# A warm-up of 9 wide multiplies becomes 7 wide and 26 narrow fp32 ones

## The chip, the cores and the metric

The kernel runs on one core of a Trainium2 chip. The metric is the device time of one execution in microseconds (us). Before the change the median of three runs is 491.01 us (488.01 to 491.92).

## The reference

Eight heads of a linear recurrence over 768 steps for 4 batches (head size 48), and then an MLP of 384 to 2048 to 384 with an exact GELU on each of the 3072 tokens:

```
for t in range(S):                       # per batch b and head h
    cur = outer(u * k_t, v_t)
    y_t = r_t @ (state + cur)
    state = w[:, None] * state + outer(k_t, v_t)
h = y @ w_in                             # (3072, 384) @ (384, 2048)
out = (0.5 * h * (1 + erf(h / sqrt(2)))) @ w_out
```

## The kernel before

The recurrence is cut into 6 chunks of 128 steps and 4 pairs of heads: 24 groups. Within a group the recurrence is a small causal attention. VectorE scales r and k by powers of the decay (`prepare`, L426); TensorE makes the scores (`scores` and `own`, L465, tile A), what the chunk adds to the state (`gains`, L476, tile UE), what the state before gives (`old`, L484, tile Y) and what the chunk's own values give (`new`, L502, tile Y); VectorE selects the causal half of the scores (L551, tile Am), advances the states (L521); ScalarE copies Y and the first states (L565, L532); GpSimd multiplies the keys by decays (L433, tile N). The first four groups, g0 to g3 here, run alone at the start, up to about 35 us. After that TensorE runs the MLP, 96 steps of 9 plus 9 multiplies of 512 columns (L649, tile Hp, and L692, tile O), and the other 20 groups between them.

The order on each engine is written out ahead by a planner (`Plan`): every piece of work has an engine, an estimated length in ns, a due time and the names that it reads and writes. Each engine then runs its list in that order. Where the planner sees TensorE idle in the first four groups, it puts multiplies by a tile of zeros (`heat`, L312) whose results nobody reads: 512 columns into UE up to the first `gains`, then 256 columns into AE. They are part of the fixed list.

At the very start stands `warm_up`, 9 multiplies of zeros with 512 columns (L314 to L320), followed by 4 of the planner's into UE; the first scores (g0) wait for VectorE's scaled T. Loads are issued on SyncE's queue, at most two or three at a time: T0, T1, N0, T2, N1, T3, w0 (the weights of the first MLP step), N2, N3, w1 and so on.

TensorE runs each multiply as a pair of instructions, a weight load (LDWEIGHTS) and the multiply (MATMUL). A multiply in plain fp32 appears in the trace as two pairs, so the 16 multiplies of `scores` are 32 pairs there; those of zeros and of the MLP are in fp32r and appear as one pair.

Of the kernel before, what the change touches and what calls it, by code (L numbers as in the profile page):

```python
# [9 lines left out]
F32 = mybir.dt.float32  # L10
# [10 lines left out]
B, H, S, D = 4, 8, 768, 48  # L21
# [17 lines left out]
LATER = 10 ** 7  # L39
FIRST, STEP, STEP_LAST = 23000, 8400, 3900  # L40
WEIGHT_AHEAD, GROUP_AHEAD, GROUP_DUE = 12500, 28000, 20000
HEATS, HEAT_NS, HEAT_ROOM = 9, 400, 300
LOADS = ("t0", "t1", "n0", "t2", "n1", "t3", "w0", "n2", "n3", "w1", "t4", "w2", "n4")
UNDERWAY, START = 2, 10
URGENT, WORTH = 1000, .5
# [6 lines left out]
class Plan:  # L52
# [9 lines left out]
    def add(self, eng, ns, at, fn, r=(), w=()):  # L62
        n = len(self.ops)
        deps = set()
        for x in r:
            deps.add(self.writer.get(x))
            self.readers.setdefault(x, []).append(n)
        for x in w:
            deps.add(self.writer.get(x))
            deps.update(self.readers.pop(x, ()))  # L70
            self.writer[x] = n
        deps -= {None, n}
        self.ops.append((eng, ns, at, fn, deps))
        self.reads.append(set(r))
# [77 lines left out]
def rwkv_gelu_mlp(tc, rkT, rkv, wuT, uN, wmlp, r, k, vT, w, u, out):  # L152
    nc = tc.nc
    with ExitStack() as ctx:
# [7 lines left out]
        def sb(shape, dt, name, pool=None):  # L162
            return (pool or wk).tile(shape, dt, name=name)
# [6 lines left out]
        AE = pso.tile([128, 2, 512], F32, name="AE")  # L170
# [34 lines left out]
        zeros = sb([128, 512], F32R, "zeros", pro)  # L205
# [4 lines left out]
        add, dma = plan.add, plan.dma  # L210
# [71 lines left out]
        for dst, src, x in ((diag2, diag, "diag"), (past2, past, "past")):  # L282
            for h in range(2):
                add("act", 280, LATER, lambda dst=dst, src=src, h=h: nc.scalar.copy(
                    out=dst[64 * h:64 * h + 64], in_=src[64 * h:64 * h + 64, 64 - 64 * h:128 - 64 * h]),
                    r=[x], w=[f"{x}2{h}"])
# [9 lines left out]
        for i in range(NP, NP + 2):  # L296
            for h in range(2):
                add("act", 520, LATER, lambda i=i, h=h: nc.scalar.copy(
                    out=flat2(T[i])[32:64, 512 * h:512 * h + 512], in_=zeros.bitcast(F32)[32:64]),
                    r=["zeros"], w=[f"T{i}"])  # L300
# [10 lines left out]
        def heat(dst, n=512):  # L311
            nc.tensor.matmul(dst, lhsT=zeros[:, 0:128], rhs=zeros[:, 0:n], start=True, stop=True)  # L312

        def warm_up():  # L314
            for n in range(HEATS):
                heat((A + [YU[:, 0], YU[:, 1]] + [AE[:, 0], AE[:, 1]])[n % 6])
            plan.filler = lambda: heat(UE[:, 1]), "O0", HEAT_NS, HEAT_ROOM
            plan.heat = lambda: heat(AE[:, 0, 0:U0], U0), 110, SHARE

        add("pe", 430 * HEATS, 10, warm_up, r=["zeros"], w=["H", "A0", "A1", "O0", "O1", "Y0", "Y1"])  # L320

# [628 lines left out]
```

## Time and profile before

| what | value |
|---|---|
| median of 3 runs | 491.01 us |
| lowest and highest run | 488.01 and 491.92 us |
| profiled execution, its own time | 492.2 us |
| span of the profiled execution | 490.5 us |
| mean granted TensorE clock | 0.993 |
| busy: TensorE multiplies, weight loads | 479.8 us, 389.8 us |
| busy: VectorE, ScalarE, GpSimd | 265.9, 174.9, 64.8 us |
| instruction packets on DMA queue 8 | 42, 0.69 MB |

The span is what the profile covers, from the first to the last instruction; 1.7 us of the execution's own time lie outside it. In the chain of waits, "issue" is time in which an engine waited for nothing that the profile shows. A granted clock of 1.00 is 2.4 GHz, 0.50 is 1.2 GHz.

### The profile page before, as it was taken

To read this page: it belongs to the slowest core of one execution; us is meant where nothing else is said; L and a number is where in the kernel's file an instruction comes from. 1 tells how busy PE (TensorE), PEld (TensorE's weight loads), DVE (VectorE), ACT (ScalarE), POOL (GpSimd) and SP (SyncE) were. 2 spreads that over 40 slices of the span, in tenths; PEclk is the share of its full clock that TensorE was granted. 3 is DMA by queue.
4 is the path that set the end of the run, shared out by engine and by line. 5 is a ranking of instruction groups with operands and counts; after the bars stand their busy time and mean duration, and the time that the engine had idled before them with its cause. 6 is when DMAs were issued, how large, how long until landed. Compare 5 with 4: busy or idle time off the path is not lost.

```text
span 490.5 us, 11672 instructions
## 1 busy us (share of the span) xinstructions
PE 479.8 (98%) x5094; PEld 389.8 (79%) x5094; DVE 265.9 (54%) x432; ACT 174.9 (36%) x353; POOL 64.8 (13%) x85
## 2 busy tenths in 40 slices
PE   8799999999999999999999999999999999999996
PEld 6687787878888888778878888888888887888885
DVE  7478989876636636536545645554545423322223
ACT  6288889853132232231321331331421311211111
POOL 5200000002202022112022021120120200000000
PEclk9799999999999999999999999999999999999999
DMA  8674576513312312303113403123313000100002
GB/s 221 210 234 170 176 268 198 193 37 113 91 31 62 92 34 77 131 0 94 43 49 94 143 3 94 33 60 93 103 42 94 1 11 13 66 0 0 1 0 71
DMA packets 13193, 42.25 MB, mean 86 GB/s; under 512 B 2160, under 2 KB 2544, under 8 KB 13136
## 3 DMA queue, kind: packets, MB, share of 16 engines
q1 hardware_dynamic: 13136, 41.43, 28.1%
q8 instruction: 42, 0.69, 0.6%
q14 instruction: 15, 0.12, 0.1%
HBM read 34.74 MB, written 4.72 MB: 80 GB/s over the span
## 4 chain that ended last, share of the span: by engine, by line
PE 96%; DVE 1%; issue 1%; DMA 1%; ACT 0%; SPq 0%; DVEq 0%
PE Hp L649 41%; PE O L692 40%; PE A L465 3%; PE Y L484 3%; PE Y L502 2%; PE AE L312 2%; PE Y L476 2%; PE Y L692 1%; DMA T<-in_rkT_dram 1%; DVE T L426 0%; PE Y L515 0%; PE UE L476 0%; DVE Am L551 0%; DVE wa L865 0%; PE A L312 0%
## 5 line engine op out<-in xcount | busy, mean ns | idle before, releaser
L649 PE MATMUL Hp<-xx,wh 128*128 128x512 f32 x576 | 166.6, 396 | 0.5 <-ACT gf L679 0.3
L679 ACT ACTIVATE gf<-Hp 128x512 f32<-128x512 f32 x96 | 57.4, 598 | 229.2 <-PE Hp L649 223.6
L680 DVE CAST gh<-gf 128x512 fp32r<-128x512 f32 x95 | 45.5, 479 | 168.4 <-ACT gf L679 167.6
L649 PEld LDWEIGHTS Hp<-xx,wh 128*128 128x128 f32 x576 | 106.8, 188 | 25.8 <-ACT gf L679 1.2
L649 PE MATMUL Hp<-xx,wl 128*128 128x512 f32 x288 | 83.3, 396 | 0.0
L692 PE MATMUL O<-gh,wh 128*128 128x512 f32 (+1 forms) x285 | 81.9, 394 | 0.0
L692 PE MATMUL O<-gl,wh 128*128 128x512 f32 (+1 forms) x285 | 80.7, 390 | 0.0
L692 PE MATMUL O<-gh,wl 128*128 128x512 f32 (+1 forms) x285 | 80.6, 390 | 0.0
L681 DVE TENSOR_TENSOR gl<-gf,gh 128x512 fp32r<-128x512 f32 x95 | 73.2, 771 | 9.7 <-DVE gh L680 0.5
L649 PEld LDWEIGHTS Hp<-xx,wl 128*128 128x128 f32 x288 | 54.0, 188 | 12.9
L692 PEld LDWEIGHTS O<-gh,wh 128*128 128x128 f32 x285 | 52.5, 188 | 12.6 <-issue 0.3
L692 PEld LDWEIGHTS O<-gl,wh 128*128 128x128 f32 x285 | 52.5, 188 | 11.6
L692 PEld LDWEIGHTS O<-gh,wl 128*128 128x128 f32 x285 | 52.5, 188 | 11.6
L456 ACT ACTIVATE Am<-diag,cs 128x64 f32<-128x64 f32 x120 | 31.7, 337 | 29.8 <-DVE cs L451 29.8
L430 POOL TENSOR_TENSOR Nb<-Nb 128x384 f32<-128x384 f32 x15 | 15.9, 1063 | 127.9 <-DMA Nb<-in_rkv_dram 112.7
L433 POOL TENSOR_TENSOR Nb<-Nb,WN 128x384 f32<-128x384 f32 x20 | 21.5, 1073 | 56.3 <-DMA Nb<-in_rkv_dram 32.0
L426 DVE TENSOR_TENSOR Tb<-Tb,E 112x1024 f32<-112x1024 f32 x20 | 25.2, 1258 | 3.2 <-DMA Tb<-in_rkT_dram 3.0
L521 DVE SCALAR_TENSOR_TENSOR Sb<-Sa,E,Y 48x192 f32<-48x192 f32 x40 | 16.5, 413 | 14.0 <-ACT xx L565 7.7
L493 POOL MEMSET turn<- 1x1 f32 x19 | 1.7, 89 | 129.2 <-PE Y L484 129.2
L565 ACT CAST xx<-Y 112x512 fp32r<-112x512 f32 (+1 forms) x18 | 10.6, 587 | 22.4 <-PE Y L476 16.4
L551 DVE COPY_PREDICATED Am<-past,A 128x512 f32<-128x512 uint32 x24 | 17.7, 736 | 0.4
L448 POOL TENSOR_TENSOR Nb<-Nb,u_sb 128x384 f32<-128x384 f32 x15 | 17.3, 1155 | 0.1
(109 smaller groups left out, 401.1 us busy)
## 6 DMA issues: line engine op xcount, KB each, us to landing
raw<-in_wmlp_dram SPq DMA_DIRECT2D x16, 768.0 KB, 4.3
Nb<-in_rkv_dram SPq DMA_DIRECT2D x15, 576.0 KB, 4.0
Tb<-in_rkT_dram SPq DMA_DIRECT2D x40, 192.0 KB, 3.5
out_dram<-raw SPq DMA_DIRECT2D x5, 768.0 KB, 3.8
Nb<-in_rkv_dram SPq DMA_DIRECT2D x5, 384.0 KB, 3.7
xx<-x SPq DMA_DIRECT2D x30, 64.0 KB, 2.3
N<-in_rkv_dram SPq DMA_DIRECT2D x4, 384.0 KB, 6.4
T<-in_rkT_dram SPq DMA_DIRECT2D x2, 448.0 KB, 4.8
```

What stands on the lines that cost most here:

```text
L426: add("dve", sdve(1024), LATER if g.gi else -10 ** 5, lambda: nc.vector.tensor_tensor(out=flat, in0=flat, in1=E[:, 0, g.p].rearrange("l h ...
L430: add("pool", pool(DM), LATER, lambda: nc.gpsimd.tensor_tensor(out=g.n[:, 0], in0=g.n[:, 0], in1=g.n[:, 1], op=ALU.mult), r=[g.K], w=[g.R])
L433: it = nc.gpsimd.tensor_tensor(out=g.kn, in0=g.kn, in1=WN[:, g.p].rearrange("s j d -> s (j d)").unsqueeze(1).to_broadcast([C, NB, 2 * D]), ...
L448: add("pool", pool(DM), LATER, lambda: nc.gpsimd.tensor_tensor(out=g.n[:, 0], in0=g.n[:, 0], in1=u_sb[:, g.p, :].unsqueeze(1).to_broadcast ...
L456: add("act", sact(HALF) + 60, LATER, lambda x=x, b=b: nc.scalar.activation(out=g.am[:, x, b, :], in_=diag2, func=AF.Copy, scale=g.sums[:, ...
L521: return nc.vector.scalar_tensor_tensor(out=g.s[h + 1][quarter(1 - x)], in0=g.s[h][l], scalar=E[l, 1, g.p, h, MID:MID + 1], in1=gained(g, ...
L551: add("dve", 722, LATER, lambda: nc.vector.copy_predicated(out=g.am, mask=mask.bitcast(U32).unsqueeze(1).unsqueeze(1).to_broadcast([C, 2, ...
L649: nc.tensor.matmul(O[3], lhsT=wt[j][:, 0, k_ * 128:(k_ + 1) * 128], rhs=x[:, a, k_, :], start=start and k_ == ks[0], stop=stop and k_ == k ...
L679: add("act", 600, LATER, lambda: nc.scalar.activation(out=gf, in_=O[3], func=AF.Gelu), r=["H"], w=["gf"])
L680: add("dve", sdve2(512), LATER, lambda: nc.vector.tensor_copy(out=high, in_=gf), r=["gf"], w=[GH])
L681: add("dve", sdve(512), LATER, lambda: nc.vector.tensor_tensor(out=low, in0=gf, in1=high.bitcast(F32), op=ALU.subtract), r=["gf", GH], w=[GL])
L692: nc.tensor.matmul(bank(dst)[:, a:b], lhsT=wt[j][:, 1, d * 128:(d + 1) * 128], rhs=gt[:, a:b], start=(j == 0 and n == 0), stop=(j == NJ - ...
```

## The change

Two of the nine wide multiplies go; after the other seven come 26 multiplies by the same zeros, read as fp32, with 64 rows, 64 weight columns and 16 moved columns, each in one of four quarters of the array, into AE. The planner is told 40 ns for each. No other code changes.

```diff
-HEATS, HEAT_NS, HEAT_ROOM = 9, 400, 300
+HEATS, SMALL, HEAT_NS, HEAT_ROOM = 7, 26, 400, 300
...
         def warm_up():
             for n in range(HEATS):
                 heat((A + [YU[:, 0], YU[:, 1]] + [AE[:, 0], AE[:, 1]])[n % 6])
+            z = zeros.bitcast(F32)
+            for n in range(SMALL):
+                i, j = (slice(64 * (n // k % 2), 64 * (n // k % 2) + 64) for k in (1, 2))
+                nc.tensor.matmul(AE[j, n % 2, 0:16], lhsT=z[i, 0:64], rhs=z[i, 0:16], start=True, stop=True)
             plan.filler = lambda: heat(UE[:, 1]), "O0", HEAT_NS, HEAT_ROOM
             plan.heat = lambda: heat(AE[:, 0, 0:U0], U0), 110, SHARE
 
-        add("pe", 430 * HEATS, 10, warm_up, r=["zeros"], w=["H", "A0", "A1", "O0", "O1", "Y0", "Y1"])
+        add("pe", 430 * HEATS + 40 * SMALL, 10, warm_up, r=["zeros"], w=["H", "A0", "A1", "O0", "O1", "Y0", "Y1"])
```

TensorE's list from the first multiply to the second group's `own`, before (T_102 and T_103 are T of g0 and g1, KB their keys times u, N_110 the keys and values of g0):

```order
1 L312 MATMUL A<-zeros 128x512 x2
2 L312 MATMUL Y<-zeros 128x512 x2
3 L312 MATMUL AE<-zeros 128x512 x2
4 L312 MATMUL A<-zeros 128x512 x2
5 L312 MATMUL Y<-zeros 128x512
6 L312 MATMUL UE<-zeros 128x512 x4
7 L465 MATMUL A<-T_102 64x64 x16
8 L312 MATMUL UE<-zeros 128x512
9 L355 MATMUL AE<-ident,E 128x112 x4
10 L465 MATMUL A<-T_102,KB_108 64x64 x16
11 L312 MATMUL UE<-zeros 128x512 x3
12 L476 MATMUL UE<-N_110 48x48 x16
```

The same list now (the lines after the edit are four higher):

```order
1 L312 MATMUL A<-zeros 128x512 x2
2 L312 MATMUL Y<-zeros 128x512 x2
3 L312 MATMUL AE<-zeros 128x512 x2
4 L312 MATMUL A<-zeros 128x512
5 L320 MATMUL AE<-zeros 64x16 x26
6 L312 MATMUL UE<-zeros 128x512 x4
7 L469 MATMUL A<-T_102 64x64 x16
8 L312 MATMUL UE<-zeros 128x512
9 L359 MATMUL AE<-ident,E 128x112 x4
10 L469 MATMUL A<-T_102,KB_108 64x64 x16
11 L312 MATMUL UE<-zeros 128x512 x3
12 L480 MATMUL UE<-N_110 48x48 x16
```

Only the warm-up's rows differ. Every later row of TensorE, down to the last, stands in the same order with the same number of zero multiplies, and so do all rows of VectorE, ScalarE, GpSimd and SyncE.

The place where the first four groups go on, g1's scores to the zero multiplies behind g0's `new`, as it stands now (it is the same before, with lines four lower):

```order
13 L469 MATMUL A<-T_103 64x64 x16
14 L469 MATMUL A<-T_103,KB_109 64x64 x16
15 L488 MATMUL Y<-T_102,Sb 48x64 x8
16 L506 MATMUL Y<-Am_116,N_110 48x64 x16
17 L312 MATMUL AE<-zeros 128x256 x8
```

In the trace each of the first four rows is twice as many pairs (32, 32, 16, 32). They stand 100 instructions further from the start than before.

## Rows read from the trace of the kernel before

**Rows 1.** The page: busy time, granted clock in 40 slices, instruction packets

```profile
PE 479.8 (98%) x5094; PEld 389.8 (79%) x5094; DVE 265.9 (54%) x432; ACT 174.9 (36%) x353; POOL 64.8 (13%) x85
...
PEclk9799999999999999999999999999999999999999
...
q8 instruction: 42, 0.69, 0.6%
```

**Rows 2.** Chain of waits, first 46 us: start us, us, what

```profile
11.09 1.16 PE A L465 x64
12.25 0.44 PE Y L484 x16
...
12.78 0.55 PE Y L502 x24
13.33 3.46 issue
16.80 0.46 PE Y L502 x8
17.26 2.00 PE AE L312 x8
19.26 1.92 PE A L465 x64
21.18 1.36 PE AE L312 x5
22.54 0.81 PE UE L476 x32
23.35 1.15 PE AE L312 x8
...
27.60 0.36 PE UE L476 x32
27.95 1.39 PE AE L312 x10
```

**Rows 3.** Stretches: length, busy us (count) by engine, granted clock, DMA share, GB/s

```profile
8.00:10.00 2.00, 1.92 (x39) 1.22 (x37) 1.87 (x4) 1.33 (x3) 1.02 (x1) 1.00 0.99 246
...
16.00:18.00 2.00, 1.20 (x12) 1.06 (x13) 0.00 (x0) 0.67 (x2) 0.00 (x0) 0.59 0.07 29
18.00:20.00 2.00, 2.00 (x35) 1.78 (x37) 0.00 (x0) 0.72 (x2) 0.87 (x1) 0.50 0.49 126
```

**Rows 4.** DMA queues from 14.5 to 15.6 us: packets, MB, share

```profile
q8 instruction: 1, 0.02, 5.6%
```

**Rows 5.** DMA queues from 18 to 19.5 us

```profile
q8 instruction: 1, 0.02, 5.9%
```

**Rows 6.** Stretches from the start to each of two stops of TensorE

```profile
0.00:13.50 13.50, 11.07 (x221) 8.41 (x221) 10.25 (x25) 8.41 (x19) 7.09 (x14) 1.00 0.83 231
...
0.00:106.20 106.20, 99.57 (x1623) 81.00 (x1624) 84.13 (x132) 80.21 (x122) 14.91 (x25) 0.97 0.62 195
```

**Rows 7.** Chain of waits, 100 to 110 us

```profile
106.02 0.39 issue
```

**Rows 8.** TensorE in order of time, first 12 us

```profile
4.29 1.05 PE L312 MATMUL A<-zeros 128*128 128x512 f32 x2
5.15 0.63 PE L312 MATMUL Y<-zeros 128*128 128x512 f32 x1
...
6.86 0.69 PE L465 MATMUL A<-T 48*64 48x64 f32 x32
...
8.31 0.69 PE L465 MATMUL A<-T,KB 48*64 48x64 f32 x32
...
10.06 0.57 PE L476 MATMUL UE<-N 64*48 64x48 f32 x32
```

**Rows 9.** VectorE in order of time, from 9 us

```profile
9.48 0.72 DVE L551 COPY_PREDICATED Am<-diag,A 128x512 f32<-128x512 uint32 x1
```

**Rows 10.** GpSimd in order of time, from 8 us

```profile
19.13 1.97 POOL L433 TENSOR_TENSOR N<-N,WN 128x384 f32<-128x384 f32 x2 [6.14 <-DMA N<-in_rkv_dram]
```

## Prediction
> **What bounds the kernel now.** I read the page's busy times first: TensorE multiplies for 98% of the span, on one core, with a granted clock of 0.9 or more in every slice but one, the second [rows 1]. From some 38 us on nothing but TensorE's own work stands on the chain, so time is to be had only ahead of that, and there the clock slice says where to look: about 12 to 25 us. The chain of waits for that stretch [rows 2] shows one large hole. g0's `new` (L502) has done 24 of its 32 pairs at 13.33 us and does nothing for 3.46 us, waiting for nothing that the profile names, in the middle of 32 identical multiplies. It goes on at 16.80. Behind that hole the granted clock is down: 0.59 on average from 16 to 18 us and 0.50 from 18 to 20 [rows 3]; the page's third slice, which begins at 24.5 us, has it up again [rows 1]. So nearly all of the work from 16.80 to about 24 us runs at the 1.2 GHz level.
>
> What ends the hole? The DMA queues by stretch show the first packet of the instruction queue between 14.5 and 15.6 us [rows 4], and TensorE starts 1.2 us after that. I read the hole as TensorE out of instructions. The counts support it. At the stop TensorE has run 221 pairs, 442 instructions [rows 6]. A second, short stop of the same kind, 0.39 us, stands at 106.02 us, again inside a run of equal multiplies [rows 7], after 1623 multiplies and 1624 weight loads [rows 6]. The difference is 2805 instructions, 11 times 255, and with the few waiting instructions that these counts leave out a block of 256 fits. A packet is 0.69 MB / 42 = 16.4 KB [rows 1]. So blocks end at a fixed count of instructions, and TensorE stops at such an end where the next block is not there.
>
> **The change part by part.** *Removed:* two wide multiplies, 0.43 us each by their starts (4.29 to 5.15 for two, [rows 8]): 0.86 us of TensorE. *Added:* 26 fp32 multiplies, 52 pairs. No row has a pair with 16 columns; the nearest are the 64-column pairs of the scores, 64 in 1.92 us at the low clock and in 1.16 us at the high one [rows 2], so 30 or 18 ns. The warm-up's wide multiplies take 0.43 us for 512 columns, the pace of the low level, though the clock reads 1.00 [rows 6, 8]; so I take 30 ns: 1.56 us, net +0.70 us; at 18 ns +0.08 us. Since the four multiplies behind them then meet a clock that has risen, I put g0's scores 0.3 us later (0 to 0.7). That is off the path: the first selection on VectorE, which the chain goes through, starts at 9.48 us [rows 9] and the scores that it needs end at 9.00 [rows 8], a cover of 0.48 us. Cost 0, or 0.2 at the upper end. If the clock stays low until g0 is done, the cover is gone and it costs about 1 us.
>
> *Moved:* 52 - 2 = 50 pairs, 100 instructions, so every block's end falls 50 pairs earlier in the work. The stop after pair 221 becomes one after what was pair 171. Counting the list (13 + 32 + 1 + 4 + 32 + 3 + 32 + 32 = 149 up to g1's scores), that is the 22nd pair of g1's `own`: at 11.09 + 54/64 x 1.16 = 12.07 us [rows 2].
>
> *When the next block comes* decides all. The stop's row alone doesn't say when it was asked for. I take it that a block is asked for when TensorE is through with the block before the one it is in, 128 pairs earlier: pair 93, the 8th of g0's `gains`, at 10.2 us [rows 8]. From there to 16.80 are 6.6 us, with the DMA engines full. The second packet fits: TensorE enters the next block at 16.80 and the packet lies between 18 and 19.5 [rows 5] with the DMA engines nearly idle (0.07, [rows 3]); with the same 1.2 us behind it that makes 3.9 us. These are my bounds: 3.9 us idle, 6.6 us loaded.
>
> Now pair 93 is the 30th of g0's scores (63 + 30), at about 7.5 us. The block would be there between 11.4 and 14.1 us and is wanted at 12.07: a stop of **0 to 2.0 us**. The DMA share from 8 to 10 us is 0.99 [rows 3], so the loaded end is nearer; I take 1.2. The block after that is wanted 128 pairs on, at old pair 299, the end of g2's `own`. TensorE's work up to there at full clock is 0.18 + 0.44 + 0.09 + 0.73 + 1.11 + 1.16 = 3.7 us [rows 2], against 3.9 to 6.6: a stop of **0.2 to 2.9**. It is asked for at about 13.3, and the loads that fill the DMA engines were done by 16 (0.07 after that, [rows 3]); I take 1.0. The third has some 4.5 us of work ahead of it: 0 to 2.1, and I take 0, as the DMA engines are then lightly loaded.
>
> *What is at stake:* the 3.46 us, and the slow clock after it. At the low clock the steps from 16.80 to 24.50 take 0.46 + 2.00 + 1.92 + 1.36 + 0.81 + 1.15 = 7.70 us [rows 2]. At the high one: 0.18 (8/24 of 0.55), 1.11 (8/10 of 1.39), 1.16, 0.70, 0.36, 1.11 = 4.62 [rows 2]. That is 3.08 us; together **6.5 us**. Shorter stops should leave the clock up: up to 13.5 us TensorE was idle for 2.4 us in all, in pieces, and the clock stayed at 1.00 [rows 6]. From 24.5 on all moves rigidly, as TensorE has no gap. What is late next is GpSimd's N2 and N3, done from about 20.1 to 21.1 because their load was late [rows 10]; g2's `gains` would want N2 at 27.60 - 6.5 = 21.1, so just no wait. The later block ends move by 50 pairs too; the 0.39 us stop may go and another come, which I count as nothing (0.4 either way).
>
> *Sum:* -6.5 + 1.2 + 1.0 + 0 = -4.3 us on the profiled execution's 492.2 us (span 490.5 and 1.7 around it): 487.9. The median of the runs, 491.0, is 1.2 below the profiled one, and the lowest, 488.0, suggests that not every run pays the whole 6.5; by the median it would be 486.7. I say **487.5**.
>
> *A rule that speaks against it.* The hole lies at pair 221 while a 16.4 KB packet arrives [rows 4, 6]. The Trainium skill, "Runtime: NRT & Kernel Launch", section "Instruction fetch mechanics", says that instructions are refilled in blocks of 256 and that crossing a block's end is mostly hidden, because the sequencer issues slower than blocks arrive. The trace agrees with the block and not with "hidden": 256 small instructions here take some 3.7 us of work and a block 3.9 or more. By that rule the hole would have another cause and nothing would move: 491.
>
> **The rivals.**
> - *Clean:* both blocks arrive in time (idle latency). All 6.5 us go: 485.7 by the profiled time, 484.5 by the median; 485. For it: 3.9 us from 7.5 is 11.4. Against it: the DMA engines are at 0.83 from the start to 13.5 us [rows 6]. Chance 0.2.
> - *The hole only moves:* 2.0 us at g1's `own`, 1.0 later, and the clock falls all the same (3.1): 0.4 us saved, 490.6 to 491.8. For it: the loaded latency is the one that I have measured at that place. Against it: 2.0 us is much shorter than the stop after which the clock fell. Chance 0.18.
> - *Slower:* the early groups now eat blocks as fast as they come, so that each of three block ends stops TensorE at the loaded price, 2.0 + 2.9 + 2.1, with the low clock between them, 3.1: 10.1 against 6.5, so 3.6 us more, 494.6 to 495.8. It decides at g2's `own`: if the block asked for at about 14 us isn't there by 19. With the 1 us of an uncovered warm-up it passes 1%. Chance 0.06.
> - *Not what it says:* the stop isn't tied to the count (a wait for data that the profile does not name), or the narrow multiplies are fewer instructions than I count; nothing moves: 491. For it: no row shows when a block is asked for. Against it: the 2805 instructions between the two stops. Chance 0.06.
>
> **How the numbers follow.** My case, a smaller stop and no fall of the clock, has 0.5 and spans 486 to 489.5. About 1% (4.9 us, so 486.1 and 495.9) is what can be told from no change. Faster: the clean case, 0.2, and a third of mine, 0.17: 0.37. Slower: half of the slower case and some unseen trouble: 0.05. The rest, 0.58, within 1%. The range from 484.6 to 491.6 leaves out the slower case and the ends of the others.
>
> **What would show it.** In the changed kernel's chain the 3.46 us in L506 are gone, and "issue" of 0 to 2 us stands at g1's `own` (L469, 22 of 32 pairs), perhaps another at g2's; the first instruction packet lies at 10 to 13 us instead of 14.5; the granted clock is 1.00 from 14 to 24 us; the first MLP step (L653) starts some 4 us earlier. Wrong if a stop stays in g0's `new`, if the clock is at 0.50 anywhere from 13 to 24, or if g0's scores start after 7.6 us.

## The result, and the profile after

The changed kernel is slower: 494.96 us median against 490.08 us for the one before, run beside it; ratio 1.0095, 95% interval 1.0069 to 1.0121. The prediction was 487.5 us with a range of 484.6 to 491.6, so it was wrong in sign as well as in size. The profiled execution took 494.96 us, with a span of 493.2.

The page shows TensorE as busy as before, and its granted clock at 0.9 or more in all slices but the fifth, 49 to 62 us, where it was the second [rows 1]:

```profile
PE 481.8 (98%) x5144; PEld 390.2 (79%) x5144; DVE 266.4 (54%) x432; ACT 175.1 (35%) x353; POOL 64.5 (13%) x85
...
PEclk9999899999999999999999999999999999999999
```

5144 multiplies instead of 5094: fifty pairs more, as the change was read. The chain of waits of the first 36 us (start us, us, what) answers to [rows 2]:

```profile
4.93 1.61 PE AE L320 x52
6.54 2.00 PE UE L312 x4
8.54 1.06 PE A L469 x32
...
10.86 0.67 PE A L469 x32
...
16.97 1.15 PE A L469 x61
18.12 1.19 issue
19.30 0.33 PE A L469 x3
...
28.06 0.65 PE Y L506 x28
28.71 0.45 issue
29.16 0.32 PE Y L506 x4
...
33.52 1.63 PE Hp L653 x6
```

The 3.46 us in g0's `new` are gone. "Issue" now stands in g2's `own`, after 61 of 64 pairs, and in g2's `new`. The 26 narrow multiplies took 1.61 us as 52 pairs, and in TensorE's timeline g0's scores came at 8.47 instead of 6.86 us [rows 8], because the four wide multiplies behind the narrow ones still ran at about half pace (0.50 us each), as did the first 32 scores (1.06 us, where the next 32 took 0.67). The first MLP step begins at 33.52 us, 1.65 us earlier than in the chain of the profile before:

```profile
35.17 1.63 PE Hp L649 x6
```

All of that is lost again within 20 us. The chain from 48 us, the DMA queue from 48.2 to 49.3 us, and then the same MLP step in the chain before:

```profile
48.36 0.16 PE Y L480 x13
48.52 1.96 issue
50.48 0.48 PE Y L480 x19
...
52.12 3.61 PE Hp L653 x9
55.73 2.10 PE O L696 x9
```

```profile
q8 instruction: 1, 0.02, 5.2%
```

```profile
51.57 2.37 PE Hp L649 x9
53.94 2.10 PE O L692 x9
```

In the middle of a run of 32 equal pairs TensorE stops for 1.96 us, and an instruction packet arrives during the stop. After it nine MLP multiplies take 3.61 us; the same nine took 2.37 before. The stretches show why (length, busy us and count by engine, granted clock, DMA share, GB/s):

```profile
52.00:54.00 2.00, 1.94 (x6) 1.49 (x6) 1.97 (x4) 2.00 (x4) 0.00 (x0) 0.50 0.13 44
```

The granted clock is 0.50, 1.2 GHz, after the stop. And the end of the kernel differs. These are the last barrier's instructions, first those of before and then those of the changed kernel (engine, count, first and last start in us; each engine's second wait ends the kernel; TensorE's first DRAIN is its last instruction ahead of the first wait):

```profile
L947 ACTq EVENT_SEMAPHORE  x2: 17/17/17, 489.9 to 490.4; - x2
...
L947 PEldq EVENT_SEMAPHORE  x2: 51/51/51, 489.9 to 490.4; - x2
```

```profile
L951 PEldq DRAIN  x2: 8/10/13, 489.4 to 493.0; - x2
L951 ACTq EVENT_SEMAPHORE  x2: 17/17/17, 491.5 to 493.2; - x2
...
L951 PEldq EVENT_SEMAPHORE  x2: 51/51/51, 492.9 to 493.2; - x2
```

Before, ScalarE and TensorE come to it together, at 489.9 us. Now ScalarE is there at 491.5 and TensorE only at 492.9, 1.4 us later, though it has nothing left to compute. An instruction packet lies in the stretch from 489.5 to 491.5 us. So the profile's balance is -1.65 at the first MLP step, +1.96 for the stop, +1.5 for the clock behind it (the next products begin at 55.73 us against 53.94, so with the lead of 1.65 us 3.44 were lost there), about -0.4 for the stop at 106 us, which is gone [rows 7], and +1.4 at the barrier: +2.8, and the execution is 2.76 us longer than the profiled one before.

### The profile page after: what moved, and what is told of

Its sections match the earlier page's. It is cut to its first block, busy times and chain, and to the rows that moved or that the text cites. A ratio compares the mean times of both kernels' runs of the same rounds, so it can differ in the third digit from the quotient of the medians.

```text
span 493.2 us, 11772 instructions
## 1 busy us (share of the span) xinstructions
PE 481.8 (98%) x5144; PEld 390.2 (79%) x5144; DVE 266.4 (54%) x432; ACT 175.1 (35%) x353; POOL 64.5 (13%) x85
## 4 chain that ended last, share of the span: by engine, by line
PE 96%; issue 1%; DVE 1%; ACT 0%; DVEq 0%
PE Hp L653 42%; PE O L696 40%; PE A L469 4%; PE Y L488 3%; PE Y L506 2%; PE Y L480 2%; PE AE L312 1%; PE Y L696 1%; DVE Am L555 1%; PE UE L312 1%; PE A L312 1%; PE Y L519 0%; PE AE L320 0%; DVE wa L869 0%; PE UE L480 0%
```

## The experiments

Two theories stood against each other. **B (block ends):** TensorE's instructions come in blocks of 256; the 100 added ones move all block ends to other work, and those that now fall badly cost more than the first one gave. **W (warm-up):** the narrow multiplies keep the clock low at the start, and that is the loss. Each kernel was timed beside the one before.

### The order of the warm-up: 9 or 5 wide multiplies ahead of the narrow ones

```diff
-HEATS, SMALL, HEAT_NS, HEAT_ROOM = 7, 26, 400, 300
+HEATS, SMALL, HEAT_NS, HEAT_ROOM = 9, 26, 400, 300
```

> Nine wide multiplies come first, then the 26 narrow ones, then two wide: the same instructions as in the change and as many (100 more than before), only two wide ones moved ahead of the narrow ones. Theory B (block ends): the change loses at block ends of TensorE's instructions, so the stops stand at the same instructions as in the change (1.2 us in g2's own, 0.4 in g2's new, 2.0 in the gains near 48 us, 1.3 us at the last barrier), and the time is within 1 us of the change's 495.0 less what an earlier clock gives. Rival W (warm-up): the narrow multiplies hold the clock down (in the change it rose at 10.5 us instead of 6.1, and g0's scores began at 8.5 instead of 6.9). Then the clock rises near 6 us here, g0's scores begin near 7 and the first MLP step starts 1.5 to 2 us earlier than the change's 33.5; 493. If W alone were the cause of the loss, the time would be 490 or less.

Measured: 494.74 us, ratio 1.0083 (1.0056 to 1.0110). Its chain, 4 to 30 us, and a stretch behind the second stop:

```profile
12.59 0.32 issue
...
16.67 2.57 issue
19.24 0.47 PE A L469 x3
```

```profile
20.00:25.00 5.00, 5.00 (x89) 4.46 (x92) 2.62 (x5) 2.99 (x5) 0.85 (x1) 0.50 0.67 174
```

The 0.32 us stand in g1's `own`, 54 of 64 pairs in, where the prediction had put its first stop. The stop in g2's `own` is at the same instruction as in the change, 61 pairs in, and so is that near 50 us (2.13 us); but here the one in g2's `own` took 2.57 us and the clock fell to 0.50 behind it. The scores began earlier (7.31 us), and that was lost again: the first MLP step begins at 35.43 us. With five wide multiplies first:

```diff
-HEATS, SMALL, HEAT_NS, HEAT_ROOM = 7, 26, 400, 300
+HEATS, SMALL, HEAT_NS, HEAT_ROOM = 5, 26, 400, 300
```

> Five wide multiplies, 26 narrow ones, six wide: the same instructions as the change (7, 26, 4) and as the run with 9, 26, 2, in another order. Theory B: same stops at the same instructions, 495 as in those two. Rival W (the narrow multiplies hold the clock down, and that costs): the clock rises at 10 us or later and the time is 1 to 2 us above the run with nine wide ones first, 496 to 497. If the late clock of the change's profile was chance, it rises near 6 here.

Measured: 494.77 us, ratio 1.0090 (1.0054 to 1.0126). Its chain from 8 to 20 us:

```profile
8.54 1.06 PE A L469 x32
...
11.08 1.06 PE A L469 x32
...
17.92 1.08 PE A L469 x61
19.00 0.10 issue
19.09 0.33 PE A L469 x3
```

Here both halves of g0's scores run at half pace, 1.06 us for 32 pairs, where the change's second half took 0.67; but the block that g2's `own` needs is then there in time: 0.10 us of stop. Nine, seven and five wide multiplies first give 494.74, 494.96 and 494.77. So W is refuted as the cause of the loss; the run with 100 instructions at the first MLP step, below, loses as much with the warm-up of before (495.00 us). In these profiles, where the pace rises late TensorE comes later to block ends, and waits less there. How late the pace rises is not fixed by the order alone either: in the run below with the change's own warm-up TensorE's timeline (start us, us) has g0's first 32 scores in 0.69 us:

```profile
7.25 0.69 PE L469 MATMUL A<-T 48*64 48x64 f32 x32
```

### 100 or 256 instructions more, elsewhere

The warm-up of before, and narrow multiplies behind the first MLP step instead, 25 or 64 of them:

```diff
+        def pad(count):
+            z = zeros.bitcast(F32)
+            for n in range(count):
+                i, j = (slice(64 * (n // k % 2), 64 * (n // k % 2) + 64) for k in (1, 2))
+                nc.tensor.matmul(A[n % 2][j, 0:16], lhsT=z[i, 0:64], rhs=z[i, 0:16], start=True, stop=True)
...
-                        product1(x, j, n, (k_,), k_ == 0 and n == 0, k_ == 2 and n == 2) for n in range(3)],
+                        product1(x, j, n, (k_,), k_ == 0 and n == 0, k_ == 2 and n == 2) for n in range(3)] + [
+                        k_ == 2 and pad(25)],
```

> The warm-up of before; 25 narrow fp32 multiplies (50 pairs, 100 instructions) behind the first MLP step at about 37 us, where they cost some 0.9 us. Theory B: up to there all is as before (3.5 us stop in g0's new); after it the block ends stand as in the change: a stop of about 2 us in the gains near 50 us, none at 106 us, 1.3 us at the last barrier; 490.1 + 0.9 + 2.0 - 0.4 + 1.3 = 493.9, and up to 1.7 more where the clock falls after the stop. Rival W: no stop, 491.0.

Measured: 495.00 us, ratio 1.0103 (1.0069 to 1.0137). The chain of its profile near 47 us, and its last barrier:

```profile
47.34 0.16 PE Y L480 x13
47.50 2.19 issue
49.69 0.48 PE Y L480 x19
```

```profile
L958 ACTq EVENT_SEMAPHORE  x2: 17/17/17, 489.4 to 491.0; - x2
...
L958 PEldq EVENT_SEMAPHORE  x2: 51/51/51, 490.7 to 491.0; - x2
```

The stop stands behind the same 13 of 32 pairs as in the change, the one at 106 us is gone, and TensorE is 1.3 us late at the barrier. Nothing of the warm-up was touched. The multiplies themselves take 0.92 us in its chain.

> As the run with 100 more instructions at the first MLP step, but 64 narrow multiplies: 128 pairs, 256 instructions, one whole block. They cost 128 x 17 ns = 2.2 us. Theory B: all block ends fall on the same work as before, so the 0.4 us stop in the gains stands again (at about 108 us), no 2 us stop near 50 us and nothing at the last barrier: 492.3, less than with 100 instructions. Rival (more instructions cost more, wherever the blocks end): slower than the run with 100, 495 or more.

Measured, with `pad(64)`: 493.34 us, ratio 1.0068 (1.0047 to 1.0089). Near 107 us:

```profile
107.24 0.25 PE Y L480 x18
107.49 0.39 issue
107.88 0.39 PE Y L480 x11
```

With one whole block more the stop is back behind the same 18 pairs and has the same length, 0.39 us, as in the kernel before [rows 7]; there is none near 50 us, and TensorE is not late at the barrier. The 128 pairs take 1.99 us; the time rose by 3.3 (2.3 to 4.4, by the ratio), 1.3 (0.3 to 2.4) more than that, which I had not expected. In the profile the excess lies ahead of the first MLP step: from its start (34.70 us) to the end of the span (491.9) are 457.2 us, and 455.3 before, which is the 1.99 us of the pairs and no more. Why the early part was slow in this run, whose first instructions are those of before, is not shown. The medians don't tell 256 from 100 for certain (the two intervals overlap), the positions of the stops do: it is where the blocks end that counts.

### 100 instructions behind the last product

```diff
+            for n in range(25):
+                i, j = (slice(64 * (n // k % 2), 64 * (n // k % 2) + 64) for k in (1, 2))
+                nc.tensor.matmul(A[n % 2][j, 0:16], lhsT=wh[0][i, 0, 0:64].bitcast(F32),
+                                 rhs=wh[0][i, 0, 0:16].bitcast(F32), start=True, stop=True)
             for _ in range(PACE):
```

> The warm-up of before; 25 narrow fp32 multiplies (100 instructions) behind TensorE's last product, where TensorE has nothing left to do that the end waits for. Theory B: nothing moves before 484 us, and at the last barrier TensorE comes 1.3 us later because a block ends between its last two waits, as in the change: 491.4. Rival: the 1.3 us at the end of the change's profile have another cause (stores that land late); then 490.1.

Measured: 493.57 us, ratio 1.0068 (1.0039 to 1.0097): 3.3 us where I expected 1.3. The last barrier:

```profile
L955 PEldq DRAIN  x2: 8/10/13, 487.8 to 491.2; - x2
L955 ACTq EVENT_SEMAPHORE  x2: 17/17/17, 488.1 to 491.4; - x2
...
L955 PEldq EVENT_SEMAPHORE  x2: 51/51/51, 491.1 to 491.4; - x2
```

ScalarE waits 3.0 us for TensorE, which multiplied last at about 485 us, and so the rival is out. The place is right and the price was too low. TensorE's own wait, from its drain to its next instruction, is about as long in both (487.8 to 491.1 us here, 489.4 to 492.9 in the change); but here the others come to the barrier 0.3 us after that drain and there 2.1 us after it, so that less of the wait is covered. A hundred instructions that compute nothing, behind the last result, cost about 0.7%.

### The change's warm-up, and the block ends put back afterwards

```diff
-                        product1(x, j, n, (k_,), k_ == 0 and n == 0, k_ == 2 and n == 2) for n in range(3)],
+                        product1(x, j, n, (k_,), k_ == 0 and n == 0, k_ == 2 and n == 2) for n in range(3)] + [
+                        k_ == 2 and pad(39)],
```

> The change, and 39 narrow multiplies (156 instructions) behind the first MLP step: with the 100 of the warm-up one whole block, so from there on all block ends fall on the same work as before. They cost 78 x 17 ns = 1.3 us. Theory B: the 2.0 us stop near 48 us and the 1.3 us at the last barrier are gone, the 0.4 us stop near 107 is back; what is left against before is the early part alone. If the early part gains the 4.3 us of the prediction: 490.1 + 1.3 - 4.3 = 487.1. If it gains the 1.6 of the profile of the change: 489.8. If, as the run with 100 at the first MLP step against the change says, it gains nothing: 491.4 to 492.3. Rival (the later loss is not tied to where blocks end): 496, the change plus 1.3.

Measured: 491.20 us, ratio 1.0033 (1.0000 to 1.0066). TensorE's waits (us in all, times, longest), its last barrier, and a stretch:

```profile
PE A L469 <- issue: 2.3, 2, 1.7
```

```profile
L958 ACTq EVENT_SEMAPHORE  x2: 17/17/17, 488.9 to 489.4; - x2
...
L958 PEldq EVENT_SEMAPHORE  x2: 51/51/51, 488.9 to 489.4; - x2
```

```profile
19.00:22.00 3.00, 3.00 (x42) 2.69 (x43) 2.29 (x4) 0.89 (x3) 1.01 (x1) 0.52 0.89 274
```

The 2 us stop and the late barrier are gone, as B says. (The 0.39 us stop near 107, which I expected, did not come back: 0.01 us stands there, at 105.55. A block there can be in time or just late.) The 78 pairs take 1.28 us, and by the ratio the time rose by 1.6 (0.0 to 3.2), so the early part gains 1.28 - 1.6 = -0.3 us (-2.0 to 1.3): nothing that can be told. Two stops, 0.59 and 1.74 us, stand in g1's and g2's `own`, and 3 us of low clock behind the second.

### Half as many

```diff
-HEATS, SMALL, HEAT_NS, HEAT_ROOM = 7, 26, 400, 300
+HEATS, SMALL, HEAT_NS, HEAT_ROOM = 9, 13, 400, 300
```

> Nine wide multiplies, then 13 narrow ones (26 pairs), one wide multiply fewer behind them: 50 instructions more than before. Theory B: the block ends fall on other work again; by the work between block ends and some 4 us for a block, no stop of over 0.5 us is left after 40 us (neither the 2.0 us near 48 nor the 0.4 at 106) and nothing at the last barrier; the early stop is between 0.5 and 2.5 us, at g0's old or new. 486 to 489. Rival W, or noise: as before, 490.

Measured: 489.14 us, ratio 0.9988 (0.9964 to 1.0012): no different from before, 5.8 us below the change by the medians, and just above the 486 to 489 that I expected. TensorE's waits in its profile (487.8 us), and the stretch from 6 to 30 us:

```profile
PE Hp L653 <- DVE gl L685: 0.7, 1, 0.7
...
PE Y L506 <- issue: 0.3, 1, 0.3
PE Y L488 <- issue: 0.2, 1, 0.2
PE UE L480 <- issue: 0.2, 1, 0.2
```

```profile
6.00:30.00 24.00, 22.64 (x665) 18.99 (x661) 18.49 (x30) 14.27 (x27) 5.53 (x5) 1.00 0.81 240
```

Three short stops, the clock at 1.00 throughout, and the first MLP step at 30.59 us, 4.6 earlier than in the profile before. The wait of 0.7 us in an MLP step at 48 us lies at the 256-instruction spacing too, though the profile puts it down to VectorE. So a wait of over 0.5 us is left behind 40 us after all, and the early stops are below the 0.5 to 2.5 that I expected. This is the picture that I had predicted for the change; but by the ratio it is worth only 0.6 us (1.8 less to 0.6 more).

## Why the prediction was wrong

- *The hole is a block's end.* Right, and now shown: in every run that adds instructions the stops move by as many, and 256 bring the 0.39 us one back to the same multiply. Counted with the waiting instructions, all these stops ahead of the last barrier, in all nine profiles, stand behind 449 + 256 k of TensorE's recorded instructions (449 and 3265 in the profile before, 11 x 256 apart; 1985 for the one of 1.96 us), and each ends 1.2 to 1.6 us after the end of an instruction packet. The wait at the last barrier is not on this count (it stands behind 10329 in the change). It, too, ends 1.3 to 1.4 us after an instruction packet in the five kernels with 100 instructions more; in the other four TensorE goes on within 0.5 us of the packet's end. That a block ends there is read from this and not counted out.
- *The first stop.* Right in kind: the block was there in time, or nearly (nothing at g1's `own` in the change's profile; 0.32 and 0.59 in two others), below the 1.2 that I took. The first packet lies between 10.5 and 12.2 us in the change's profile, as forecast.
- *The second stop, at g2's `own`.* I said 0.2 to 2.9 and took 1.0: 1.19 in the change, and 2.57, 1.74 and 0.10 in the three other runs with the same block ends. Behind the two longest the clock fell, so "shorter stops should leave the clock up" failed at 1.74 us, and at 1.56 behind g0's `new` in the run with 100 instructions at the first MLP step. The length alone does not settle it: behind that run's stop of 2.19 us nine MLP multiplies took 2.37 us, as before, and behind the change's 1.96 us 3.61. The third stop, in g2's `new`, which I took at 0 (0 to 2.1), was 0.45 in the change and 0.72 with five wide multiplies first.
- *What is at stake, 6.5 us.* Too large, and with it the forecast gain of 4.3 us. It is the price in one execution. Three runs that begin exactly as before show what g0's `new` costs elsewhere: 2.78, 1.56 and 1.24 us. Their first MLP steps begin at 34.70, 31.65 and 32.49 us, with 35.17 in the profile before: 33.5 on average. Those with the change's block ends begin at 33.52, 35.43, 33.58 and 33.51: 34.0. The early part gains nothing that these runs can tell; that the change's own profile gained 1.65 us there is luck of the draw.
- *"The later block ends move by 50 pairs too; the 0.39 us stop may go and another come, which I count as nothing."* This is the step that failed, and it turned the sign. The stop that came is 1.96 us (2.13, 2.19 and 2.46 in the other runs with these block ends), with 1.5 us of low clock behind it in the profile, and the last barrier waits 1.4 us for a block (1.0 to 1.3 in the others). The run with 100 instructions at the first MLP step prices it by the ratio: 0.0103 x 490.13 - 0.92 = 4.1 us (2.5 to 5.8), though the uneven early part is in that too. The profiles price it without them. From the start of the first MLP step to the end of the span, less the multiplies added there, are 454.7 to 455.5 us in the four kernels without this stop and the late barrier (before, half as many, 256, the change with 156 later), and 458.5 to 459.7 in the four with both (the change, nine and five wide, 100 at the first MLP step); the means are 4.1 us apart. The sum had -4.3 us and the ratio says +4.7: these 4.1 and the 4.3 of the early part that did not come are nearly all of the difference. I had looked at block ends where the change was and not where else they fell.
- *The warm-up at no cost.* The narrow multiplies' price was right (1.61 us against 1.56), the cover was not: g0's scores came 1.6 us later, at 8.47, which was a sign of being wrong (after 7.6 us), and g1's began at 13.25 us in the chain, 2.2 later than before [rows 2]. That this cost nothing in the end is argued and not shown: where g1's scores came early (11.55 us with nine wide multiplies first, 11.49 with 156 later), the stop in g2's `own` was longer (2.57 and 1.74 us), and the first MLP step no earlier.
- *The rule of the Trainium skill* in "Runtime: NRT & Kernel Launch", "Instruction fetch mechanics", that a block's end is mostly hidden, holds behind blocks of the MLP alone: between two block ends at 456.3 and 481.7 us of the profile before lie 25.4 us (some 110 pairs at 0.23 us, 2.10 for nine, and waiting instructions), and there is no stop. It does not hold everywhere in these runs: the stops stand where the block ahead had run in 1.8 to 4.8 us.
- *The rivals.* "Slower" had the right sign and the right cause, blocks late by their count, and the wrong place: I put it into the first 20 us and gave it 0.06. That its 494.6 to 495.8 us holds the measured 494.96 is luck.

Left open: why the same block takes so different a time. g0's `new` stopped for 1.24 to 3.46 us at the same instruction behind the same loads; the stop in g0's `new` lies where the DMA engines are full (0.95 from 14 to 16 us in the profile before), but no run took the loads away. What differs is when the packet comes: in the four profiles that begin as before it starts at 11.7, 12.1, 13.4 and 14.6 us, takes 1.0 to 1.5 us, and TensorE goes on 1.2 to 1.4 us after its end. Why it starts so differently is not shown, nor when it was asked for.

## What to carry to other kernels

Where an engine's instructions are short, count them: adding some anywhere moves every later end of a block of instructions, to the last barrier. Before such a change, list the work at each block's end and how long the block ahead of it runs; in these nine profiles TensorE stopped only behind blocks of 256 that had run in 1.8 to 4.8 us. Not behind all such: the one that ended at 27.5 us in the profile before had run in 3.1 us, and TensorE did not stop. And a stall in one profile is one draw: its length there is not what the median pays.

## What the runs showed of the hardware that I had not expected

An engine that has finished can hold up the end: with 100 idle instructions behind the last product the barrier waited 3.0 us for TensorE. The low clock outlasts its cause: after a stop of 1.96 us the granted clock was 0.50 from 52 to 54 us with TensorE busy for 1.94 of the 2.00. And the granted clock as the profile shows it does not tell the pace at the start: from 8 to 10 us the change's profile shows 1.00 while 32 scores took 1.06 us, as against 0.69 in other runs. The trace's first entry of the clock, a rise to full speed, stands at 10.49 us there (at 6.14 in the profile before, at 14.61 with five wide multiplies first), and ahead of it the 1.00 rests on no entry:

```profile
8.00:10.00 2.00, 2.00 (x35) 1.36 (x34) 1.83 (x3) 0.00 (x0) 0.00 (x0) 1.00 0.86 199
```
